# One core, an attention with dilated window beside a state-space scan: a spin on TensorE, a new load order, masks on GpSimd, the scan in two halves and a new order of units

## The chip, the cores and the metric

The kernel runs on one NeuronCore of a Trainium2 chip. The metric is device time of one execution in microseconds (us), lower is better. PE is TensorE, PEld its weight loads, DVE VectorE, ACT ScalarE, POOL GpSimd, SP SyncE, which here issues nearly all DMAs.

## The reference

Two independent computations on sequences of S = 2048 rows with D = 448 features; their outputs stand side by side in the last axis.

```
q, k, v = heads of x @ wqkv                  # A: 16 heads of 28
idx = pos - (0, 2, ..., 14)                  # 8 keys, every second one back
attn = softmax(where(idx >= 0, q . k[idx] * 28**-0.5, -1e9))
a = (attn @ v[idx]) @ wo
Bu = x @ B_bar.T                             # B: complex, 448 states
h[t] = Lam_bar * h[t-1] + Bu[t]
b = 2 * real(h @ C.T) + x * Dskip
```

## The kernel before, in words

**Parity.** All windows step by two, so even and odd rows are kept apart: rows are viewed as 1024 pairs (NK = 1024). xA and xB are loaded transposed (features on partitions), the even half in their first tiles and the odd half in the last ones.

**Attention.** For each parity, `proj_qk` makes 16 units (4 matmuls of 512 columns each, into qT or kT) and `proj_v` 9 units (4 of 448 columns, into Vp). `att_round` is one of 12 rounds per parity (3 query ranges by 4 head groups): 12 mask matmuls (mkB against mkA) and 12 score matmuls into the PSUM tile S, one exponential on ACT into P, 12 matmuls with Vp into av, and a copy into oT. There is one S tile and one av tile. `normalise` sends the sums of each range through DRAM (n1, n2), takes a reciprocal on DVE (n3), sends it back broadcast (n4, n5: inv_b) and multiplies (n6). `wo_block` is the output projection of 128 pairs.

**Scan.** lB is built from Bn and the parameters (`lBa` on ACT, `lBb` on DVE, line 480), transposed on PE and copied into VW (`vwt`, `vwe`). `state_in` (7 matmuls of 512 columns, line 709) makes 14 units, copied into Hs. `scan` turns the complex recurrence into two real ones: it multiplies by tables of cosine and sine (tab, made by POOL products and an ACT sine), runs `tensor_tensor_scan` over 1024 pairs (line 736) and rotates back. There are three such blocks of 128 states and a last one with 64. `y_block` multiplies by CwO and CwEK, which are built from C on ACT and DVE (line 805); `k0` makes the term of the same pair.

**What sets the order.** Nothing in the program is scheduled by hand on the engines: class `Plan` holds every piece as an `Op` with an engine, a duration, dependences and a rank. `run` simulates, takes the lowest rank among what can start, and then emits the instructions in that order. Each engine then executes its own list strictly in that order. Evacuations of PSUM (`evac`) go to ACT or DVE as the plan finds them free. Three PSUM tiles ("mm") turn round for projections, transposes and outputs. Output tiles are four ("yo").

**Start.** SP issues the loads in the order of the `load` calls. ACT issues 13 small DMAs for the parameters, which are laid out one value per partition. DVE builds mkA and mkB in fp32 in some thirty steps (lines 312 to 356). A flag, computed at the end, would start a slow exact path; it does not.

Of the kernel before, what the change touches and what calls it, by code (L numbers as in the profile page):

```python
# [17 lines left out]
QB = 121  # L18
NB = 9
# [15 lines left out]
class Plan:  # L35


    HOP = 0.12
# [10 lines left out]
    def run(self):  # L49
# [4 lines left out]
        while todo:  # L54
            cand = {}
            for op in todo:
                t = 0.0
                for d in op.deps:
                    if d.end is None:
                        t = INF  # L60
                        break
                    t = max(t, d.end + d.lat + (self.HOP if d.ran != op.eng else 0.0))
# [66 lines left out]
def main_part(ctx, tc, A_x, A_wqkv, A_wo, B_x, B_Lambda_re, B_Lambda_im, B_B_re, B_B_im, B_C_re, B_C_im, B_log_dt,  # L129
# [44 lines left out]
    phs = T([128, 4, NK], I32, "oT")  # L174
# [21 lines left out]
    par_raw = T([128, 3, 4], BF16, "par_raw")  # L196
    dsk_raw = T([128, 2, 4], BF16, "dsk_raw")
# [3 lines left out]
    L = {}  # L201

    def load(name, at, q, fn):
        L[name] = P.add(name, q, 0.06, fn, rank=-1000 + len(L), lat=at)

    xA_r = A_x[0].rearrange("(k j) d -> k (j d)", j=2)
    xB_r = B_x[0].rearrange("(k j) d -> k (j d)", j=2)

    for i, vec in enumerate((B_Lambda_re, B_Lambda_im, B_log_dt)):
        def f(i=i, vec=vec):  # L210
            ACT.dma_start(par_raw[:, i, 0:3], vec[0:384].rearrange("(t i) -> i t", i=128))
            ACT.dma_start(par_raw[0:64, i, 3:4], vec[384:448].rearrange("(i o) -> i o", o=1))
# [22 lines left out]
    def bload():  # L235
# [4 lines left out]
        SP.dma_start(Bm[0:64, :], B_B_im[384:448])  # L240
        SP.dma_start(Bm[64:128, :], B_B_re[384:448])
# [12 lines left out]
    load("xA_E0", 4.2, "SP", lambda: xpose(xA, xA_r, 0, 4, 0, 512))  # L254
    for kt in range(4):
        n = 128 if kt < 3 else 64
        load(f"W_Eqk{kt}", 4.5 + 0.6 * kt, "SP",
             lambda kt=kt, n=n: SP.dma_start(raw[0][0:n, kt, 0:D2], A_wqkv[128 * kt:128 * kt + n, 0:D2]))
    load("xA_E1", 9.0, "SP", lambda: xpose(xA, xA_r, 0, 4, 512, 1024))
    load("Bn", 12.0, "SP", bload)  # L260
    load("W_Ev", 13.5, "SP", lambda: wload(0, wv[0], D2, D3))
    load("xB0", 17.0, "SP", lambda: xpose(xB, xB_r, 0, 7, 0, 512))
    load("xB1", 20.0, "SP", lambda: xpose(xB, xB_r, 0, 7, 512, 1024))
    load("xA_O", 24.0, "SP", lambda: xpose(xA, xA_r, 4, 7, 0, 1024))
    load("W_Ov", 26.0, "SP", lambda: wload(1, wv[1], D2, D3))
    load("W_Oqk", 28.0, "SP", lambda: wload(1, raw[1], 0, D2))
    load("wo", 31.0, "SP", woload)
    load("C", 3.0, "SP", cload)
# [4 lines left out]
    o_id = P.add("ident", "POOL", 1.0, c0, rank=-898.5)  # L273
    o_warm = None

    def c1():
        POOL.memset(raw[0][64:128, 3, :], 0.0)
        POOL.memset(raw[0][:, :, D2:900], 0.0)
        POOL.memset(wv[0][64:128, 3, :], 0.0)
        POOL.memset(wv[1][0:64, 0, :], 0.0)  # L280
    o_wz = P.add("wzero", "POOL", 1.5, c1, rank=-899)
# [15 lines left out]
    def c2():  # L297
        POOL.iota(iot, [[1, NK]], base=0, channel_multiplier=0)
    o_iota = P.add("iota", "POOL", 1.0, c2, rank=-898)

    one_i = T([128, 1], I32, "one_i")

    def c3():
        POOL.memset(one_i[:], 1 << 30)
    o_m0 = P.add("mask0", "POOL", 0.5, c3, rank=-897)
    rowi = T([128, 1], I32, "rowi")
    rowf = T([128, 4], F32, "rowf")

# [12 lines left out]

    mf = T([128, 5, 144], F32, "scr")
    mi = mf[:, 4, :].bitcast(I32)

    def c5():

        POOL.iota(mi.rearrange("p (a b) -> p a b", b=8), [[1, 18], [0, 8]], base=-1, channel_multiplier=0)
        V.tensor_copy(mf[:, 0, :], mi)
        POOL.iota(mi.rearrange("p (a b) -> p a b", b=16), [[0, 9], [1, 16]], base=-8, channel_multiplier=0)
        V.tensor_copy(mf[:, 1, :], mi)  # L330
        c = rowf[:, 2:3]
        kind = rowf[:, 1:2]
# [35 lines left out]
    o_wp0 = P.add("wpz", "POOL", 2.0, c7, rank=-898.7)  # L368
# [7 lines left out]
    f32p = T([128, 3, 4], F32, "f32p")  # L376
# [13 lines left out]

    def q1():
        V.tensor_copy(f32p[:], par_raw[:])
    o_q1 = P.add("par_f", "DVE", 0.15, q1, deps=[L["par0"], L["par1"], L["par2"]], rank=-800)
    o_q2 = P.add("dt", "ACT", 0.3, lambda: ACT.activation(dtt[:], ld, ACTF.Exp), deps=[o_q1], rank=-800)

# [12 lines left out]
    o_q3 = P.add("turns", "DVE", 1.0, q3, deps=[o_q2, o_q0], rank=-799)  # L408
# [7 lines left out]
    o_q4 = P.add("rsc", "ACT", 3.0, q4, deps=[o_q3, o_q0], rank=-799)  # L416
# [5 lines left out]
    o_q5 = P.add("lam", "DVE", 0.3, q5, deps=[o_q4], rank=-798)  # L422
# [27 lines left out]
    o_q6 = P.add("coef", "DVE", 2.8, q6, deps=[o_q5], rank=-500)  # L450
# [3 lines left out]
    for t in range(4):  # L454
        def f(t=t):
# [442 lines left out]
    for t in range(4):  # L898
        scan(t, 20 + t)
# [153 lines left out]
```

## Time and profile before

| | |
|---|---|
| time, 2 runs | 186.12 and 188.25, median 187.19 us |
| the profiled execution | 186.38 us, span 184.5 us |
| busy | PE 143.2, DVE 113.3, ACT 104.8, POOL 28.8 us |
| mean granted TensorE clock | 0.928 |

The span runs from the first to the last instruction; the 1.9 us to the device time lie around it. A busy PE is the union of its matmuls, also when they run at half clock.

### The profile page before, as it was taken

Reading aid. Unit: us, or ns where it says so; the run is one execution under the profiler, and the core shown is the slowest. Engines: PE = TensorE matmul, PEld = TensorE weight load, DVE = VectorE, ACT = ScalarE, POOL = GpSimd, SP = SyncE. Lnnn points to the kernel's source line nnn. Section 1 sums busy time; section 2 is a strip of 40 time slices with the busy share of each in tenths; the row PEclk is TensorE's granted clock in tenths of the full one; section 3 lists DMA queues with packets and bytes.
Section 4 is the critical chain, followed back from the end, with each engine's and each line's share of the span. In section 5 each row is a group of like instructions: output and inputs, shape, how many; then the busy total and the mean of one; then the engine's idle time right before and its main releaser. Section 6 shows DMA issues by size and latency. Waiting matters only on the chain.

```text
span 184.5 us, 3726 instructions
## 1 busy us (share of the span) xinstructions
PE 143.2 (78%) x1496; PEld 70.8 (38%) x1504; DVE 113.3 (61%) x219; ACT 104.8 (57%) x157; POOL 28.8 (16%) x40
## 2 busy tenths in 40 slices
PE   0039120589999999999889965599999999999870
PEld 0003020454454444444344433245444455444430
DVE  0058989987050089999999999839833323154420
ACT  0037035777696354379979956885974556312340
POOL 8805507261880000000000000000000000000000
PEclk9999855559999999999999999969999999999997
DMA  4897999900006200000000300130204311333651
GB/s 79 210 189 214 218 206 236 245 14 2 0 0 136 41 0 0 0 0 4 0 9 6 83 0 6 43 97 6 68 10 121 112 56 55 82 102 85 192 166 42
DMA packets 33173, 14.45 MB, mean 78 GB/s; under 512 B 22624, under 2 KB 33152, under 8 KB 33152
## 3 DMA queue, kind: packets, MB, share of 16 engines
q1 hardware_dynamic: 30512, 14.17, 31.5%
q10 hardware_dynamic: 2640, 0.01, 0.8%
q8 instruction: 13, 0.21, 0.5%
q14 instruction: 8, 0.07, 0.1%
HBM read 6.01 MB, written 3.80 MB: 53 GB/s over the span
## 4 chain that ended last, share of the span: by engine, by line
DVE 40%; PE 34%; DMA 11%; ACT 5%; SPq 4%; issue 4%; DVEq 0%; POOL 0%
PE mm L855 12%; DVE scr L736 7%; PE mm L538 6%; PE mm L863 4%; DMA inv_b<-inv 3%; PE mm L709 3%; DVE lB L480 3%; PE mm L683 3%; SPq L657 3%; DMA raw<-in_A_wqkv_dram 3%; DMA par_raw<-in_B_log_dt_dram 2%; DVE scr L731 2%; DVE sm L646 2%; ACT P L606 1%; DVE Hs L732 1%
## 5 line engine op out<-in xcount | busy, mean ns | idle before, releaser
L606 ACT ACTIVATE P<-S 128x1452 bf16<-128x1452 f32 (+1 forms) x24 | 31.5, 1314 | 4.0 <-PE S L597 3.9
L538 PE MATMUL mm<-xA,wqk 128*128 128x512 bf16 x63 | 17.8, 445 | 12.7 <-DVE wqk L287 12.5
L709 PE MATMUL mm<-xB,VW 128*128 128x512 bf16 x96 | 21.2, 379 | 0.1
L538 PEld LDWEIGHTS <-wqk 128*128 128x128 bf16 x64 | 6.9, 110 | 22.9 <-DVE wqk L287 13.4
L490 ACT CAST Hs<-mm 128x512 bf16<-128x512 f32 x14 | 8.2, 585 | 12.0 <-PE mm L709 12.0
L538 PE MATMUL mm<-xA,wqkO 128*128 128x512 bf16 x59 | 14.3, 380 | 0.3 <-issue 0.2
L709 PEld LDWEIGHTS <-VW 128*128 128x128 bf16 x98 | 9.6, 98 | 11.5
L683 PE MATMUL mm<-Wp,oT 128*128 128x448 bf16 x64 | 12.6, 352 | 1.6 <-DMA sm<-sum 1.0
L614 PE MATMUL av<-P,Vp 128*32 128x121 bf16 (+1 forms) x288 | 8.3, 221 | 7.0 <-DVE oT L492 4.3
L736 DVE TENSOR_TENSOR_SCAN scr<-p_r,Hs 128x1024 bf16<-128x1024 f32 x6 | 13.4, 2278 | 0.1
L855 PEld LDWEIGHTS <-Hs 128*128 128x128 bf16 x112 | 10.0, 98 | 9.1 <-issue 2.0
L855 PE MATMUL mm<-CwEK,Hs 128*128 128x448 bf16 x56 | 13.3, 355 | 0.0
L855 PE MATMUL mm<-CwO,Hs 128*128 128x448 bf16 x56 | 13.3, 354 | 0.0
L591 PE MATMUL S<-mkB,mkA 32*128 32x121 bf16 (+1 forms) x288 | 8.3, 219 | 6.4 <-DVE mkB L356 6.4
L490 ACT CAST qT<-mm 128x512 bf16<-128x512 f32 x15 | 9.0, 597 | 6.1 <-PE mm L538 6.0
L490 ACT CAST yo<-mm 128x448 bf16<-128x448 f32 x11 | 5.8, 530 | 11.1 <-PE mm L855 11.1
L492 DVE CAST oT<-av 128x363 bf16<-128x363 f32 (+1 forms) x13 | 6.4, 491 | 7.3 <-PE av L614 7.3
L614 PEld LDWEIGHTS <-Vp 128*32 128x32 bf16 x288 | 4.5, 97 | 16.3 <-issue 8.4
L731 DVE TENSOR_TENSOR scr<-Hs,tab 128x2048 bf16<-128x2048 bf16 x3 | 3.7, 1226 | 11.1 <-ACT Hs L490 10.9
L456 POOL TENSOR_TENSOR oT<-oT,F_i 128x1024 int32<-128x1024 int32 x4 | 7.8, 1942 | 16.7 <-ACT tab L461 16.7
L662 DVE TENSOR_TENSOR oT<-oT,inv_b 128x1452 bf16<-128x1452 bf16 (+1 forms) x6 | 5.2, 871 | 7.2 <-DMA inv_b<-inv 4.6
L560 PEld LDWEIGHTS <-xA 128*128 128x128 bf16 x72 | 6.7, 98 | 6.6 <-issue 0.5
(194 smaller groups left out, 259.5 us busy)
## 6 DMA issues: line engine op xcount, KB each, us to landing
out_dram<-ya SPq DMA_DIRECT2D x16, 112.0 KB, 1.7
out_dram<-yo SPq DMA_DIRECT2D x8, 224.0 KB, 2.4
inv_b<-inv SPq DMA_DIRECT2D x16, 90.8 KB, 2.9
raw<-in_A_wqkv_dram SPq DMA_DIRECT2D x3, 224.0 KB, 3.6
rawO<-in_A_wqkv_dram SPq DMA_DIRECT2D x1, 672.0 KB
inv_b<-inv SPq DMA_DIRECT2D x8, 74.5 KB, 2.2
Wp<-in_A_wo_dram SPq DMA_DIRECT2D x4, 98.0 KB
Bn<-in_B_B_re_dram SPq DMA_DIRECT2D x1, 336.0 KB
```

Source lines behind the costliest of these rows:

```text
L456: POOL.tensor_tensor(phs[:, 1, :], iot, F_i[:, t:t + 1].to_broadcast((128, NK)), ALU.mult)
L490: ACT.copy(dst, src)
L538: PE.matmul(ps[:], Wt[:, j, c:c + 128], xA[:, t0 + j, 512 * blk:512 * blk + 512], start=(j == 0), stop=(j == 3))
L591: PE.matmul(ps[:, i, c:c + n], mkA[p, :], mkB[p, mk:mk + n], start=(c == 0), stop=False, skip_group_check=True)
L606: ACT.activation(pt[:, :, 0:nq], hold["S"][:, :, 0:nq], ACTF.Exp, scale=float(DH) ** -0.5)
L614: PE.matmul(av[32 * i:32 * i + 32, c:c + n], Vp[:, par * NB + b, 4 * g + i, :], hold["P"][:, i, c:c + n], start=True, stop=True, skip_grou ...
L683: PE.matmul(ps[:, 0:D], oT[:, g, par, cols], Wp[:, g, :], start=(g == 0), stop=(g == 3))
L709: PE.matmul(ps[:], VW[:, kt, m, :], xB[:, kt, 512 * blk:512 * blk + 512], start=(kt == 0), stop=(kt == 6))
L731: step("sa", 1.15, lambda: V.tensor_tensor(scr[:], vv, sinb, ALU.mult))
L736: step(f"se{i}", 2.3, lambda i=i: V.tensor_tensor_scan(scr[:, i], r2[:, t:t + 1].to_broadcast((128, NK)), vv[:, i], 0.0, ALU.mult, ALU.add))
L855: PE.matmul(ps[:, 0:D], Hs[:, m, off:off + 128], Cw[:, m, :], start=(m == 0), stop=(m == 6))
L863: PE.matmul(ps[:, 0:D], xB[0:n, j, c0:c0 + 128], CwEK[0:n, 7 + j, :], start=False, stop=False)
```

## The change

- **Spin and parameters.** DVE clears a tile; PE runs 10 matmuls of 512 columns on zeros, then two transposes of the parameters, then two more such matmuls, and only then the first projection. The parameters come by 4 DMAs of 7 rows by 64 values.
- **Loads.** The first x transposes are halved (256 rows), the value weights go ahead of the query and key weights. Bm is copied from Bn by DVE instead of loaded.
- **Masks.** mkA and mkB are made for 32 partitions by 9 `affine_select` and 3 memsets on POOL, and copied to the others by DVE.
- **Scan.** Hs becomes two tiles of 512 pairs. `scan` runs for each half: rotate in, scan, carry (the last state, rotated by the table's entry 512, is the start value `ini` of the second half), rotate out. Tables have 514 columns instead of 1024, in two buffers.
- **Order.** Ranks are new throughout (value units first, state units among attention rounds, attention of the odd parity among y blocks), durations and hop costs of the plan too.

```diff
-    HOP = 0.12
+    HOP = {"PE": 0.28, "SP": 0.05}
...
+    o_z = P.add("zt", "DVE", 0.3, lambda: V.memset(zt[:], 0.0), rank=-2000)
+    P.add("warm0", "PE", 4.2, warm(10), deps=[o_z], rank=-2000)
+    def q0a():
+        ps = ps_mm.tile([128, 28], BF16, tag="mm", name="mmp")
+        hold_w["par"] = ps
+        for h in range(2):
+            PE.transpose(ps[64 * h:64 * h + 64, :], par_raw[:], ident[0:28, 0:28])
+    o_pt = P.add("part", "PE", 0.2, q0a, deps=[L["par3"], o_id], rank=-1999, take="mm")
+    P.add("warm1", "PE", 0.9, warm(2), deps=[o_pt], rank=-1998)
...
+        POOL.affine_select(f, f, u16, ALU.is_gt, NEG, base=0, channel_multiplier=-1)
...
-            POOL.tensor_tensor(phs[:, 1, :], iot, F_i[:, t:t + 1].to_broadcast((128, NK)), ALU.mult)
+            POOL.tensor_tensor(phs[:, b + 1, :], iot, F_i[:, t:t + 1].to_broadcast((128, TB)), ALU.mult)
...
+            def run(i):
+                V.tensor_tensor_scan(scr[:, i], r2[:, t:t + 1].to_broadcast((128, HK)), vv[:, i],
+                                     ini[:, t, i:i + 1] if blk else 0.0, ALU.mult, ALU.add)
+            def carry():
+                e = scr[:, :, HK - 1:HK]
+                TT(ini[:, t, 2:4].unsqueeze(2), e, tab[:, t, 1:2, HK:HK + 1].to_broadcast((128, 2, 1)), ALU.mult)
...
-        state_in(m, blk, -100 + 2 * i + blk)
+            state_in(m, blk, 28 + 1.5 * (7 * blk + i))
...
-                proj_qk(0, blk, g, w, -300 + 20 * blk + 2 * g + w)
+                proj_qk(0, blk, g, w, 9 + 9 * blk + 2 * g + w)
...
-        proj_v(0, b, -240 + b)
-        proj_v(1, b, 100 + b)
-    for t in range(4):
-        scan(t, 20 + t)
+        proj_v(0, b, 5 + b if b < 4 else 15 + b)
+        proj_v(1, b, 58 + b)
+    for blk in range(2):
+        for t in range(4):
+            scan(t, blk, 40 + 20 * blk + 0.1 * t)
```

What stands on SP's queue first, before: xA, the even x, then raw (query and key weights), Bn, and late wvE (value weights).

```order
L224 DMA_TRANSPOSE xA<-in_A_x_dram 128x4x512
L258 DMA raw<-in_A_wqkv_dram 128x896 x3
L258 DMA raw<-in_A_wqkv_dram 64x896
L224 DMA_TRANSPOSE xA<-in_A_x_dram 128x4x512
L236 DMA Bn<-in_B_B_re_dram 128x3x448
...
L240 DMA Bm<-in_B_B_im_dram 64x448
L241 DMA Bm<-in_B_B_re_dram 64x448
L229 DMA wvE<-in_A_wqkv_dram 128x3x448
```

The same queue after the change:

```order
L224 DMA_TRANSPOSE xA<-in_A_x_dram 128x4x256
L229 DMA wvE<-in_A_wqkv_dram 128x3x448
L230 DMA wvE<-in_A_wqkv_dram 64x448
L224 DMA_TRANSPOSE xA<-in_A_x_dram 128x4x256
L258 DMA raw<-in_A_wqkv_dram 128x896 x3
L258 DMA raw<-in_A_wqkv_dram 64x896
L224 DMA_TRANSPOSE xA<-in_A_x_dram 128x4x512
L236 DMA Bn<-in_B_B_re_dram 128x3x448
```

The value weights moved to second place; query and key weights and Bn stand behind them.

DVE, where the first scan block begins, before (scr is the scratch of the scan, Hs the states):

```order
L492 CAST Vp<-mm 128x16x28 x3
L731 TENSOR_TENSOR scr_646<-Hs,tab 128x2048
L732 TENSOR_TENSOR Hs<-Hs,tab 128x2x1024
L733 TENSOR_TENSOR Hs<-Hs,scr_646 128x1024
L734 TENSOR_TENSOR Hs<-Hs,scr_646 128x1024
L736 SCALAR_TENSOR_TENSOR scr_646<-p_r_114,Hs 128x1024 x2
```

The same place after the change, up to where other work comes in between (CwO, the output matrix, and a state unit):

```order
L502 COPY VW<-mmt 128x384 x3
L746 TENSOR_TENSOR scr_681<-Hs_93,tab 128x1024
L747 TENSOR_TENSOR Hs_93<-Hs_93,tab 128x2x512
...
L752 SCALAR_TENSOR_TENSOR scr_681<-p_r_115,Hs_93 128x512 x2
L757 TENSOR_TENSOR ini<-scr_681,tab 128x2
...
L768 COPY Hs_94<-Hs_93 128x2
...
L856 SCALAR_TENSOR_TENSOR CwO<-CT,cfO,ctmp_136 128x448
L502 CAST Hs_94<-mm 128x512
```

The scan now starts right behind the VW copies, in half lengths. All value and all query and key units of the even parity still stand ahead of the state units on PE; from there on state units, attention rounds and DVE's scan run side by side.

## Rows read from the trace of the kernel before

**Rows 1.** The page: busy time, and two lines of 40 slices of 4.6 us

```profile
PE 143.2 (78%) x1496; PEld 70.8 (38%) x1504; DVE 113.3 (61%) x219; ACT 104.8 (57%) x157; POOL 28.8 (16%) x40
...
PEclk9999855559999999999999999969999999999997
...
GB/s 79 210 189 214 218 206 236 245 14 2 0 0 136 41 0 0 0 0 4 0 9 6 83 0 6 43 97 6 68 10 121 112 56 55 82 102 85 192 166 42
```

**Rows 2.** Busy time by stretch: length, PE, PEld, DVE, ACT, POOL, clock, DMA

```profile
11.50:40.60 29.10, 14.25 (x97) 7.88 (x99) 26.81 (x89) 15.05 (x26) 11.43 (x12) 0.67 0.87 198
40.60:58.40 17.80, 17.58 (x83) 8.22 (x83) 7.11 (x16) 13.91 (x18) 9.49 (x7) 0.96 0.09 20
58.40:80.30 21.90, 21.80 (x133) 9.99 (x133) 14.68 (x13) 9.72 (x18) 0.00 (x0) 1.00 0.12 22
80.30:105.00 24.70, 22.84 (x338) 11.12 (x336) 24.13 (x25) 22.34 (x35) 0.00 (x0) 1.00 0.08 18
105.00:120.00 15.00, 8.95 (x206) 5.09 (x208) 14.06 (x28) 10.68 (x18) 0.00 (x0) 1.00 0.06 18
120.00:170.00 50.00, 49.57 (x621) 24.57 (x614) 22.36 (x46) 28.20 (x40) 0.00 (x0) 0.97 0.26 70
170.00:179.00 9.00, 8.23 (x43) 3.96 (x41) 3.12 (x6) 3.63 (x7) 0.00 (x0) 1.00 0.62 180
```

**Rows 3.** Timeline of PE, first 60 us: start, length, instructions

```profile
11.57 1.46 PE L538 MATMUL mm<-xA,wqk 128*128 128x512 bf16 x3 [11.57 <-DVE wqk L287]
...
40.63 10.75 PE L538 MATMUL mm<-xA,wqk 128*128 128x512 bf16 x46 [0.22 <-issue]
51.21 4.70 PE L560 MATMUL mm<-wvE,xA 128*128 128x448 bf16 x24
...
58.38 1.89 PE L709 MATMUL mm<-xB,VW 128*128 128x512 bf16 x7
```

**Rows 4.** Timeline of DVE, first 60 us

```profile
11.02 0.17 DVE L392 CAST f32p<-par_raw 128x12 f32<-128x12 bf16 x1 [11.02 <-DMA par_raw<-in_B_log_dt_dram]
...
15.49 0.17 DVE L407 TENSOR_SCALAR F_i<-p_fr 128x4 int32<-128x4 f32 x1
...
16.32 1.92 DVE L334 TENSOR_SCALAR scr<-scr,rowf 128x128 f32<-128x128 f32 x1
...
25.25 0.23 DVE L356 TENSOR_SCALAR mkB<-scr 128x128 bf16<-128x128 f32 x1
```

**Rows 5.** Groups by line and shape: count, busy us and mean ns, idle before

```profile
L480 DVE SCALAR_TENSOR_TENSOR lB<-Bn,p_lamr,ctmp 128x448 bf16<-128x448 bf16 x7 | 7.4, 1092 | 0.0
...
L805 DVE SCALAR_TENSOR_TENSOR CwO<-CT,cfO,ctmp 128x448 bf16<-128x448 bf16 x7 | 4.5, 672 | 0.0
...
L492 DVE CAST Vp<-mm 128x448 bf16<-128x448 f32 x3 | 1.9, 624 | 0.3
...
L287 DVE COPY wqk<-raw 128x1024 bf16<-128x1024 bf16 x4 | 1.5, 420 | 0.0
```

**Rows 6.** The chain that ended last: start, length, piece

```profile
7.04 3.75 DMA par_raw<-in_B_log_dt_dram
...
65.24 1.24 DVE scr L731
...
77.51 1.24 DVE scr L731
...
159.81 0.20 PE mm L859 x4
...
163.63 0.20 PE mm L859 x4
...
173.41 5.47 PE mm L683 x28
```

**Rows 7.** Timeline of POOL

```profile
4.54 0.29 POOL masks.py:199 TENSOR_SCALAR_AFFINE_SELECT ident<-ident 128x128 bf16<-128x128 bf16 x1
...
16.22 1.93 POOL L456 TENSOR_TENSOR oT<-oT,F_i 128x1024 int32<-128x1024 int32 x1
```

More of the change, by code (lines that the diff above doesn't have):

```diff
@@ L278, in c1 @@
         POOL.memset(raw[0][:, :, D2:900], 0.0)
-        POOL.memset(wv[0][64:128, 3, :], 0.0)
-        POOL.memset(wv[1][0:64, 0, :], 0.0)
-    o_wz = P.add("wzero", "POOL", 1.5, c1, rank=-899)
+    o_wz = P.add("wzero", "POOL", 1.0, c1, rank=-897.5)
+    o_wv = [P.add(f"wvz{i}", "POOL", 0.47, lambda i=i: POOL.memset(wv[i][64 - 64 * i:128 - 64 * i, 3 - 3 * i, :], 0.0),
+                  rank=-899 if i == 0 else -880) for i in range(2)]
     o_rp = [[], []]
@@ L359, in c6 @@
+        POOL.affine_select(c, c, [[0, 144]], ALU.is_ge, 0.0, base=-16, channel_multiplier=1)
+    o_m0 = P.add("mask0", "POOL", 3.5, c3, rank=-600)
+    def c5():
+        V.tensor_tensor(mkB[0:32, :], mk_[:, 0, :], mk_[:, 1, :], ALU.min)
+        for t in (mkA, mkB):
+            V.tensor_copy(t[32:64, :], t[0:32, :])
+            V.tensor_copy(t[64:128, :], t[0:64, :])
+    o_mask = P.add("mask2", "DVE", 0.7, c5, deps=[o_m0], rank=-100)
     def c6():
@@ L389, in main_part, with warm, f @@
     o_q0 = P.add("sg", "POOL", 0.4, q0, rank=-895.5)
-    def q1():
-        V.tensor_copy(f32p[:], par_raw[:])
-    o_q1 = P.add("par_f", "DVE", 0.15, q1, deps=[L["par0"], L["par1"], L["par2"]], rank=-800)
-    o_q2 = P.add("dt", "ACT", 0.3, lambda: ACT.activation(dtt[:], ld, ACTF.Exp), deps=[o_q1], rank=-800)
+    hold_w = {}
+    def warm(n):
+        def f():
+            if not hold_w:
+                hold_w["ps"] = ps_av.tile([128, 512], F32, tag="av", name="warm")
+            for _ in range(n):
+                PE.matmul(hold_w["ps"][:], zt[:, 0:128], zt[:], start=True, stop=True)
+        return f
+    o_z = P.add("zt", "DVE", 0.3, lambda: V.memset(zt[:], 0.0), rank=-2000)
[7 more added lines that the diff above has]
+    P.add("warm1", "PE", 0.9, warm(2), deps=[o_pt], rank=-1998)
+    def q1():
+        ps = hold_w["par"].rearrange("p (v c) -> p v c", c=7)
+        V.tensor_copy(f32p[0:64, :, :], ps[0:64, :, 0:7:2])
+        V.tensor_copy(f32p[64:128, :, 0:3], ps[64:128, :, 1:7:2])
+        V.tensor_copy(f32p[64:128, :, 3:4], ps[64:128, :, 6:7])
+        V.tensor_copy(dskO[0:64, 1:4], ps[0:64, 3, 1:7:2])
+        V.tensor_copy(dskO[64:128, :], ps[64:128, 3, 0:7:2])
+    o_q1 = P.add("par_f", "DVE", 0.8, q1, deps=[o_pt], rank=-990, give="mm")
+    o_q2 = P.add("dt", "ACT", 0.3, lambda: ACT.activation(dtt[:], ld, ACTF.Exp), deps=[o_q1], rank=-990)
     def q3():
@@ L494, in ecost @@
     def ecost(n):
-        return {"ACT": 0.19 + n / 1200.0, "DVE": 0.09 + n / 960.0}
+        return {"ACT": 0.17 + n / 1200.0, "DVE": 0.12 + n / 960.0}
     o_vw = {}
@@ L606, in f @@
             ACT.activation(pt[:, :, 0:nq], hold["S"][:, :, 0:nq], ACTF.Exp, scale=float(DH) ** -0.5)
-        o2 = P.add(f"X{par}{r}{g}", "ACT", 0.2 + 4 * nq / 1200.0, f, deps=[o1] + o_tab, rank=rank - 50, take="P", give="S")
+        o2 = P.add(f"X{par}{r}{g}", "ACT", 0.12 + 4 * nq / 1200.0, f, deps=[o1] + o_tab, rank=rank - 600, take="P", give="S")
         def f():
@@ L690, in f @@
             evac(e, yo[:, 0, :], hold["ps"][:, 0:D])
-        o2 = P.add(f"woe{par}{c}", AD, ecost(448), f, deps=[o1], rank=rank - 40, give="mm", take="yo")
+        o2 = P.add(f"woe{par}{c}", AD, ecost(448), f, deps=[o1], rank=rank - 500, give="mm", take="yo")
         def f():
@@ L713, in f @@
         def f(e):
-            evac(e, Hs[:, m, 2 + 512 * blk:2 + 512 * blk + 512], hold["ps"][:])
-        o_st[m, blk] = P.add(f"ue{m}{blk}", AD, ecost(512), f, deps=[o1, o_vp], rank=rank - 20, give="mm")
-    o_h = []
-    def scan(t, rank):
-        deps = [o_st[m, blk] for m in ((t, t + 3) if t < 3 else (6,)) for blk in range(2)] + [o_tab[t]]
-        last = list(deps) + o_h[-1:]
+            evac(e, Hs[blk][:, m, 2:HK + 2], hold["ps"][:])
+        o_st[m, blk] = P.add(f"ue{m}{blk}", AD, ecost(512), f, deps=[o1, o_vp], rank=rank - 500, give="mm")
@@ L723, in step, with scan @@
+    o_h = [[], []]
+    def scan(t, blk, rank):
+        deps = [o_st[m, blk] for m in ((t, t + 3) if t < 3 else (6,))] + [o_tab[t], o_vp, o_mask]
+        last = list(deps) + (o_h[0] if blk else [])
         def step(name, dur, fn):
-            o = P.add(f"{name}{t}", "DVE", dur, fn, deps=list(last), rank=rank)
+            o = P.add(f"{name}{t}{blk}", "DVE", dur, fn, deps=list(last), rank=rank)
             last[:] = [o]
-        cos, sin = tab[:, t, 0, :], tab[:, t, 1, :]
+        TT = V.tensor_tensor
+        H_ = Hs[blk]
+        cos, sin = tab[:, t, 0, 0:HK], tab[:, t, 1, 0:HK]
+        c5, s5 = tab[:, t, 0, HK:HK + 1], tab[:, t, 1, HK:HK + 1]
@@ new lines, in rot_out @@
+            def rot_out():
+                TT(vv, scr[:], cosb, ALU.mult)
+                TT(scr[:], scr[:], sinb, ALU.mult)
+                TT(vv[:, 0], vv[:, 0], scr[:, 1], ALU.subtract)
+                TT(vv[:, 1], vv[:, 1], scr[:, 0], ALU.add)
+                if blk == 0:
+                    V.tensor_copy(Hs[1][:, t:t + 4:3, 1:2], H_[:, t:t + 4:3, HK + 1:HK + 2])
+            step("sr", 2.1, rot_in)
+            step("s0", 1.2, lambda: run(0))
+            step("s1", 1.2, lambda: run(1))
@@ new lines, in rot_out @@
+            def rot_out():
+                TT(scr[:, 1, :], scr[:, 1, :], sin, ALU.mult)
+                TT(vv, scr[:, 0, :], cos, ALU.mult)
+                TT(vv, vv, scr[:, 1, :], ALU.subtract)
+                if blk == 0:
+                    V.tensor_copy(Hs[1][:, 6, 1:2], H_[:, 6, HK + 1:HK + 2])
+            step("sr", 1.6, rot_in)
+            step("s0", 1.7, run)
+            if blk == 0:
+                step("sc", 0.5, carry)
+            step("so", 1.15 + 0.15 * (1 - blk), rot_out)
@@ L923, in f @@
         PE.matmul(ps[0:1, 0:1], csum[:, 0:1], csum[:, 1:2], start=True, stop=True)
-    o2 = P.add("fl1", "PE", 0.2, f, deps=[o1, o_one], rank=190, take="mm")
+    o2 = P.add("fl1", "PE", 0.2, f, deps=[o1, o_one], rank=110, take="mm")
     def f():
         V.tensor_scalar(flag[:], hold_f["ps"][0:1, 0:1], float(H * S) - 0.5, None, ALU.is_lt)
-    P.add("fl2", "DVE", 0.1, f, deps=[o2], rank=190, give="mm")
+    P.add("fl2", "DVE", 0.1, f, deps=[o2], rank=110, give="mm")
     P.run()
```

313 lines of the change are left out of this document (146 added, 167 removed).

## The prediction

> **What bounds the kernel now.** Read the busy line and the slices of the page first. PE is busy 143.2 of 184.5 us, more than any other engine, and the line of the granted clock shows fives in slices 4 to 8; DMA traffic fills the same stretch and falls from 245 to 14 GB/s after slice 8, at about 37 us [rows 1]. So there are two kernels in one: a head in which data and parameters arrive, and a body in which PE works. The stretches give the sizes [rows 2]. From 11.5 to 40.6 us PE is busy 14.25 of 29.1 us at a mean clock of 0.67, while DVE is busy 26.8: the head is DVE's. Its timeline says why: the parameters come only at 11.02, and then the steps of the two masks stand on it from 16.32 to 25.48 [rows 4], ahead of everything that leads to VW. In the timeline of PE, 46 query and key matmuls can start only at 40.63, the value units at 51.21, the first state unit at 58.38 [rows 3].
>
> The body runs from 58.4 to 179.0 us. PE's busy times in it are 21.80 + 22.84 + 8.95 + 49.57 + 8.23 = 111.4 of 120.6 us [rows 2]; so 9.2 us are idle, 6.05 of them between 105 and 120, where DVE is busy 14.06 of 15 and PE's copies wait behind the scan in DVE's queue. The tail behind PE's last matmul, 173.41 + 5.47 [rows 6], is 184.5 - 178.9 = 5.6 us.
>
> The time is therefore: start of the first state unit + PE work from there + idle in it + 5.6, and 1.9 us around the span (186.38 - 184.5). The profiled execution is 0.8 us under the median of the runs shown, so I take its sum as it is.
>
> **The head, part by part.** *Parameters.* In the chain the last of nine DMAs of the three parameter vectors is issued at 7.04 and lands 3.75 us later [rows 6]. Four in place of thirteen are issued by 7.04 x 4/9 = 3.1 us and land at about 6.9; the two transposes and the spin stand ahead of the first value unit on PE, which has nothing to do before 11.57 anyhow [rows 3]. If the DMAs land late the value units wait behind the transposes in PE's queue; I price that at 0 to 2 us. From the first parameter step to F_i took 11.02 to 15.66 with other steps between [rows 4]; with the extra casts out of PSUM I take 3.0 us, so F_i at 9.9 instead of 15.7.
>
> *Loads.* Query and key weights now stand behind the value weights: 0.4 MB more ahead at 0.21 MB per us [rows 1] is 1.9 us later. What hides it is DVE, which behind F_i has three copies of value units (0.62 each), four of weights (0.42) [rows 5] and 0.4 us of small steps: 9.9 + 4.0 = 13.9 us for the first query and key unit, 2.3 us later than today. This edit alone loses; it pays because four value units are already done. Bn comes behind 3.05 MB, about 16.5 us after the start of transfers, still ahead of its use.
>
> *PE from 13.9 us.* Sixteen query and key units at 4 x 10.75/46 = 0.93 (14.9 us), five value units at 4.70/6 = 0.78 (3.9) [rows 3], two attention rounds (about 1.5) and the transposes for VW (4 us, an estimate from the 14.25 us that PE is busy in the head of today with 16 such matmuls, a round and all transposes). Sum 24.3: the first state unit at 38.2, against 58.4.
>
> *DVE in the same stretch.* Of today's 26.8 us, masks (9.2, and about 1.2 for their row numbers) go to POOL, parameters and weights come earlier (3.6), and lB drops from 1092 to about 672 ns apiece, the figure of the same shape in CwO (7 x 0.42 = 2.9) [rows 5]; eight more evacuations (5.0), more VW copies (1.5), diagonals, Bm and mask copies (3.4) come in, estimates from like steps. That is some 20 us: 33.9, so PE is the later one, by 4 us.
>
> *Masks on POOL.* No row shows these shapes; the nearest is the affine select of the identity, 0.29 us [rows 7], and thirteen steps are about 3.5 us, ahead of the table products, with half of today's length. What they may cost is DVE: a mask step took 1.92 us beside POOL's product of 1.93 us from 16.22, and its like 0.23 once POOL was idle [rows 4, 7]. POOL's products still sum to 8 x 0.97 = 7.8 us, so the bounds are 0 and 7.8 on DVE. With 4 us of slack there I take 1 us on the path. The Trainium skill (SBUF — State Buffer, Who interferes with whom) says that one of the two engines waits for the other's whole instruction, but not when DVE has at most one input in SBUF and runs outside its two-port modes; evacuations out of PSUM would then pass freely, the loss would stay inside the 4 us of slack, and the sum would be 1 us lower. The 1.92 us agree with its first half; for the second no row stands here.
>
> I put the first state unit at 39 us, with bounds of 36 and 44.
>
> **The body.** PE's work is today's 111.4, less about 1.0 (one round is done earlier), less 1.5 for the clock of 0.97 over 50 us [rows 2]: 108.9. The halves of the scan add nothing to PE. *DVE:* a block of two rows of states takes 77.51 - 65.24 = 12.3 us today [rows 6]. Three of these and the short one are 45; twice as many instructions, carries and copies add about 5 (an estimate of 0.07 us on some 70 instructions). Beside it the new order puts fourteen steps for CwO and CwEK (9.4), the reciprocals and products of three ranges (6, an estimate from their size beside a CwO step) and some twenty evacuations (0.62 each, 13) [rows 5] on DVE: 78 us from the first scan to the last. It starts when two state units are copied, 4 us after the first: 43 + 78 = 121. PE reaches the first y block of the second half after 108.9 less 3.5 pairs of y units (3.82 each, 163.63 - 159.81), ten output blocks (5.47/7 = 0.78 each) [rows 6] and the first y unit itself, that is 85.7 us: 39 + 85.7 = 124.7. So the halves do what they can: the scan is 4 us ahead of its reader, with PE at full work. But two engines near 100% with strict queues disturb each other, and that is the term that no row fixes. From below it is 1 us (PE from 120 to 170 idles 0.4 of 50), from above 17 (the 6.05 of 15 between 105 and 120, over half of the stretch) [rows 2]. I take 7.5, near today's 9.2, since odd-parity projections and rounds beside a busy DVE are what idled 1.86 of 24.7 us.
>
> Sum: 39 + 108.9 + 7.5 + 5.6 = 161.0, with 1.9 **162.9 us**, 13% under today.
>
> **Rivals.** *All covers hold:* idle 1 instead of 7.5, first state unit at 37: 154.4. For it speaks the full PE from 120 to 170; against it, 105 to 120. *The head's clock or POOL:* the spin ends before data come, PE idles until 13.9, and the units run at the lower level (1.2 GHz) as the head does today, with clock 0.67 [rows 2]; 18.8 us of units with a third at half clock cost 6 us; POOL's 7.8 us on DVE give about the same: 169. Against it: the units behind today's transposes lost only 0.7 us to the clock (0.96 over 17.8 us from 40.6) [rows 2]. *Lock-step, the slower one:* DVE's evacuations stand behind scan steps all through the 85.7 us, and PE works at the share of 105 to 120, 8.95/15 = 0.60: 143 in place of 85.7 + 7.5, so 213 us. It decides against the change (over 190.9) when PE's share there is under 85.7/121 = 0.71. Against it: the new order takes evacuations between the scan steps, and ACT, which shares the evacuations, is busy only 70.9 of the 111.6 us from 58.4 to 170 today [rows 2].
>
> **How the numbers follow.** Two per cent is about what a measurement of this kernel can tell from no change: 183.4 to 190.9. Chances: forecast, 157 to 167, 0.50; covers hold 0.20; head at 167 to 172, 0.18; some lock-step, 172 to 183, 0.05; within 2% 0.03; lock-step beyond 0.04. The range takes the covers' value less 1.4 and the head's case with two us of idle more: 153 to 174.
>
> **What would show it.** First value matmul at 6 to 8 us and first state unit at 36 to 42; full clock from about 17 us; DVE free of masks; between the first state unit and the first y unit of the second half PE at 90% or more; the last scan step a few us ahead of that y unit; a tail of 5 to 6. The forecast is wrong if DVE's last scan step ends after 128, if PE's share in the body is under 85%, or if the first state unit is not before 44.

## The result, and the profile after

167.25 and 168.68 us, median 167.97, against 187.19: ratio 0.897, 95% interval 0.870 to 0.925. The forecast was 162.9, its own band 157 to 167; the time lies in the band of the rival "the head's clock or POOL" (167 to 172), and in the range. The profiled execution is the one of 167.25 us, span 165.5 us.

The page after, the lines of [rows 1]:

```profile
PE 145.0 (88%) x1518; PEld 69.7 (42%) x1518; DVE 124.6 (75%) x271; ACT 92.8 (56%) x144; POOL 24.9 (15%) x49
...
PEclk9997898799999999999999999999999999997898
```

PE does the same work in 19 us less. Busy times by stretch (columns as in [rows 2]):

```profile
10.00:15.00 5.00, 1.53 (x4) 0.42 (x5) 4.96 (x11) 0.43 (x3) 4.51 (x10) 0.92 1.02 268
15.00:20.00 5.00, 5.00 (x19) 2.01 (x18) 4.79 (x19) 2.64 (x5) 3.84 (x5) 0.74 1.10 210
20.00:25.00 5.00, 2.68 (x12) 1.05 (x11) 4.87 (x12) 3.57 (x6) 3.89 (x6) 1.00 1.13 238
25.00:30.00 5.00, 3.39 (x12) 1.41 (x12) 4.67 (x16) 2.80 (x4) 0.00 (x0) 0.78 0.99 230
...
46.70:80.00 33.30, 33.30 (x371) 15.44 (x370) 28.58 (x54) 24.54 (x37) 3.98 (x4) 1.00 0.18 38
80.00:131.90 51.90, 51.90 (x767) 26.28 (x766) 49.09 (x99) 37.83 (x58) 0.00 (x0) 1.00 0.15 42
131.90:145.00 13.10, 13.10 (x89) 6.50 (x88) 6.41 (x14) 2.12 (x4) 0.00 (x0) 1.00 0.27 75
145.00:159.70 14.70, 12.45 (x55) 5.39 (x53) 6.19 (x13) 2.97 (x6) 0.00 (x0) 0.88 0.52 151
```

From 46.7 to 145 us PE is never idle, though DVE is busy 91% of the time up to 131.9. The loss is ahead of 46.7, while DVE is all but full. PE there (as [rows 3]; in brackets the idle time and what ended it):

```profile
6.43 3.19 PE L570 MATMUL mm<-wvE,xA 128*128 128x448 bf16 x16 [0.86 <-DMA wvE<-in_A_wqkv_dram]
...
14.64 6.16 PE L548 MATMUL mm<-xA,wqk 128*128 128x512 bf16 x21 [1.06 <-DVE wqk L286]
22.16 1.89 PE L548 MATMUL mm<-xA,wqk 128*128 128x512 bf16 x8 [1.37 <-DVE kT L502]
26.61 2.40 PE L548 MATMUL mm<-xA,wqk 128*128 128x512 bf16 x8 [2.57 <-DVE kT L502]
...
39.45 0.35 PE L624 MATMUL av<-P,Vp 128*32 128x121 bf16 x12 [2.10 <-ACT P L616]
...
46.67 7.72 PE L719 MATMUL mm<-xB,VW 128*128 128x512 bf16 x35
...
131.90 0.35 PE L901 MATMUL mm<-CwO,Hs 128*128 128x448 bf16 x1
...
150.51 5.62 PE L693 MATMUL mm<-Wp,oT 128*128 128x448 bf16 x20 [1.87 <-DVE flag L974]
156.52 3.19 PE L693 MATMUL mm<-Wp,oT 128*128 128x448 bf16 x16 [0.38 <-ACT ya L500]
```

Two waits, 1.37 and 2.57 us, are for casts of kT, which last 0.69 us each. DVE's timeline (as [rows 4]) tells why they come late (the 128x4 steps from L429 on, the "coefficient steps", work out cfO and cfE, the factors of CwO and CwEK):

```profile
9.47 0.25 DVE L411 TENSOR_SCALAR F_i<-p_fr 128x4 int32<-128x4 f32 x1
...
12.47 2.11 DVE L286 COPY wqk<-raw 128x1024 bf16<-128x1024 bf16 x2
14.50 1.00 DVE L429 TENSOR_SCALAR p_nr<-p_lamr 128x4 f32<-128x4 f32 x1
15.42 0.15 DVE L430 TENSOR_TENSOR p_den<-f32p 128x4 f32<-128x4 f32 x1
15.49 1.01 DVE L431 TENSOR_TENSOR p_tA<-f32p 128x4 f32<-128x4 f32 x1
...
21.42 0.69 DVE L502 CAST kT<-mm 128x512 bf16<-128x512 f32 x1
22.02 0.69 DVE L331 TENSOR_TENSOR mkB<-mk__108 32x144 bf16<-32x144 bf16 x1
22.72 1.86 DVE L333 COPY mkA<-mkA 32x128 bf16<-32x128 bf16 x1
...
25.87 0.69 DVE L502 CAST kT<-mm 128x512 bf16<-128x512 f32 x1
...
131.10 0.42 DVE L801 TENSOR_TENSOR Hs<-Hs,scr 128x512 bf16<-128x512 bf16 x1
```

Most steps of 128x4 values last 0.15 us, some 0.80 to 1.02. POOL (as [rows 7]) runs eight phase products, of which the first and the last pair are, with the memset behind them:

```profile
13.26 1.03 POOL L462 TENSOR_TENSOR oT<-oT,F_i 128x514 int32<-128x514 int32 x1
14.37 1.10 POOL L463 TENSOR_TENSOR oT<-oT,one_i 128x514 int32<-128x514 int32 x1
...
21.59 1.04 POOL L462 TENSOR_TENSOR oT<-oT,F_i 128x514 int32<-128x514 int32 x1 [0.78 <-ACT tab L467]
22.71 1.04 POOL L463 TENSOR_TENSOR oT<-oT,one_i 128x514 int32<-128x514 int32 x1
23.69 0.85 POOL L290 MEMSET rawO<- 64x900 bf16 x1
```

A long step ends when the product beside it ends: 14.50 + 1.00 against 14.37 + 1.10. The mkA copy (22.72 + 1.86) ends with the memset behind the last product (23.69 + 0.85). The casts of kT read PSUM and keep their 0.69 us even beside a product (21.42 beside 21.59).

Of the experiments, e2, e9 and e10 were profiled in an execution over 1.5% above the fastest of their kernel, so their first state units below are, if anything, late; the ratios below leave such executions out, the medians do not.

### The profile page after: what moved, and what is told of

It is laid out like the page before. It is cut to its first block, busy times and chain, and to the rows that moved or that the text cites. A ratio compares the mean times of both kernels' runs of the same rounds, so it can differ in the third digit from the quotient of the medians.

```text
span 165.5 us, 3791 instructions
## 1 busy us (share of the span) xinstructions
PE 145.0 (88%) x1518; PEld 69.7 (42%) x1518; DVE 124.6 (75%) x271; ACT 92.8 (56%) x144; POOL 24.9 (15%) x49
## 4 chain that ended last, share of the span: by engine, by line
PE 67%; DVE 14%; DMA 6%; ACT 5%; SPq 3%; issue 1%; DVEq 0%; ACTq 0%
PE mm L548 14%; PE mm L719 13%; PE mm L901 9%; PE mm L570 7%; PE mm L693 5%; PE av L624 4%; DMA inv_b<-inv 4%; PE S L601 3%; PE mm L881 3%; SPq L667 3%; PE mm L909 3%; DMA out_dram<-yo 2%; PE warm L377 2%; PE S L607 2%; DVE wqk L286 2%; ACT P L616 2%
## 5 line engine op out<-in xcount | busy, mean ns | idle before, releaser
L693 PE MATMUL mm<-Wp,oT 128*128 128x448 bf16 x64 | 15.0, 386 | 2.2 <-DVE flag L974 1.9
L548 PE MATMUL mm<-xA,wqkO 128*128 128x512 bf16 x64 | 15.5, 380 | 0.0
L500 ACT CAST yo<-mm 128x448 bf16<-128x448 f32 x9 | 4.8, 532 | 16.1 <-PE mm L901 8.8
L500 ACT CAST ya<-mm 128x448 bf16<-128x448 f32 x12 | 6.1, 535 | 12.8 <-DMA out_dram<-yo 11.5
L500 ACT CAST qT<-mm 128x512 bf16<-128x512 f32 x10 | 5.9, 586 | 9.7 <-PE mm L548 9.7
L500 ACT CAST Hs<-mm 128x512 bf16<-128x512 f32 x12 | 7.0, 586 | 7.4 <-PE mm L719 7.3
L693 PEld LDWEIGHTS <-oT 128*128 128x128 bf16 x64 | 6.4, 105 | 9.2 <-issue 4.8
L570 PE MATMUL mm<-wvE,xA 128*128 128x448 bf16 x36 | 8.6, 378 | 0.9 <-DMA wvE<-in_A_wqkv_dram 0.9
L500 ACT CAST oT<-av 128x363 bf16<-128x363 f32 (+1 forms) x18 | 8.0, 445 | 1.7 <-PE av L624 1.7
L548 PEld LDWEIGHTS <-wqkO 128*128 128x128 bf16 x64 | 5.8, 98 | 6.6
```

The source lines that it names most:

```text
L500: ACT.copy(dst, src)
L548: PE.matmul(ps[:], Wt[:, j, c:c + 128], xA[:, t0 + j, 512 * blk:512 * blk + 512], start=(j == 0), stop=(j == 3))
L570: PE.matmul(ps[:, 0:D], xA[:, t0 + j, ks:ks + 128], Wt[:, j, :], start=(j == 0), stop=(j == 3))
L693: PE.matmul(ps[:, 0:D], oT[:, g, par, cols], Wp[:, g, :], start=(g == 0), stop=(g == 3))
```

## The experiments

All were timed in five rounds (e3 three); e0 to e3 ran together, so did e4 to e7, e8 and e9, e10 and e11. "us faster" below is the difference of two ratios times 187.2.

```
run                 median us  ratio to before, 95%        first state unit (us)
e0_changed            167.56   0.8925 (0.8851-0.8999)      47.05
e1_coef_late          159.89   0.8587 (0.8552-0.8621)      40.99
e2_small_products     161.41   0.8658 (0.8615-0.8701)      41.99
e3_y_waits_both       173.49   0.9302 (0.9241-0.9363)      47.10
e4_no_spin            167.42   0.8949 (0.8896-0.9003)      46.62
e5_qk_first           170.70   0.9136 (0.9077-0.9196)      50.07
e6_tail               161.36   0.8632 (0.8576-0.8688)      40.23
e7_old_masks          170.29   0.9107 (0.9047-0.9166)      49.81
e8_norm_bufs          156.01   0.8359 (0.8310-0.8407)      40.66
e9_split_copies       158.26   0.8403 (0.8341-0.8464)      41.65
e10_norm_no_spin      155.21   0.8299 (0.8246-0.8351)      43.08
e11_spin_gap          154.42   0.8266 (0.8226-0.8307)      38.32
```

**e0.** 

> The changed kernel again, unaltered, so that the variants beside it have a time on the same chip: 167 to 169 us, ratio 0.89 to 0.905 of the kernel before, first state unit at 46 to 47 us.

As expected.

**e1: the small steps out of the casts' way.**

```diff
+    o_q6.deps.append(o_lB[-1]); o_mask.deps.append(o_ph[-1])
-    o_dg = P.add("dg", "DVE", 1.4, f, deps=[o_q1, o_id, o_dz], rank=22)
+    o_dg = P.add("dg", "DVE", 1.4, f, deps=[o_q1, o_id, o_dz, o_lB[-1]], rank=22)
```

> The coefficient steps (L429 to L453) and the diagonal matrices (L865 to L868) are made to wait for the last lB step, the mask copies (L331 to L334) for the last of GpSimd's phase products; nothing is left out. Theory (in the head, the casts of the Q/K projections stand in VectorE's queue behind small steps that GpSimd's products stretch, 7.0 us of coefficient steps and 3 us of mask steps, and TensorE waits 1.4 + 2.6 us for two kT casts): those two waits go, the first state unit comes at 42 to 43.5 us instead of 46.7, and the time falls by 3 to 4 us, unless VectorE's 4 us of work put into the body make the second half's first y unit wait, which would give 1 to 3 of them back. Rival (TensorE's head is set by the landing of the loads and by ScalarE, so that another wait is next in line): first state unit at 46 us or later, time within 1 us of the changed kernel.

6.3 us faster. PE in e1, with no wait for kT left:

```profile
14.64 10.94 PE L548 MATMUL mm<-xA,wqk 128*128 128x512 bf16 x37 [1.06 <-DVE wqk L286]
...
40.99 7.72 PE L719 MATMUL mm<-xB,VW 128*128 128x512 bf16 x35
...
144.62 3.94 PE L693 MATMUL mm<-Wp,oT 128*128 128x448 bf16 x20 [1.66 <-DVE flag L974]
150.20 3.19 PE L693 MATMUL mm<-Wp,oT 128*128 128x448 bf16 x16 [1.63 <-ACT ya L500]
```

The theory holds, and was undersized: the new order also has other units beside the first exponential, so the 2.10 us at 39.45 are gone. A cast out of PSUM that started just behind a product, in e1 on DVE and POOL:

```profile
18.70 0.69 DVE L502 CAST qT<-mm 128x512 bf16<-128x512 f32 x1 [4.12 <-PE mm L548]
```

```profile
18.61 1.04 POOL L462 TENSOR_TENSOR oT<-oT,F_i 128x514 int32<-128x514 int32 x1 [1.01 <-ACT tab L467]
```

It kept its 0.69 us.

**e2: the products shortened, the order kept.**

```diff
-            POOL.tensor_tensor(phs[:, b + 1, :], iot, F_i[:, t:t + 1].to_broadcast((128, TB)), ALU.mult)
+            POOL.tensor_tensor(phs[:, b + 1, 0:8], iot[:, 0:8], F_i[:, t:t + 1].to_broadcast((128, 8)), ALU.mult)
```

> GpSimd's eight phase products (L462, L463) are cut from 514 columns to 8, and ScalarE's sine reads one column repeated, so the rotation table is wrong; the order of the instructions on TensorE, VectorE and ScalarE is unchanged. Theory (the same instructions on VectorE are long only because GpSimd's products run beside them): no 128x4 step over 0.3 us, the coefficient steps 3 us instead of 7.0, the mkA copy 0.2 us instead of 1.86, the double wqk copy 0.8 to 1.0 us instead of 2.1, first state unit at 41.5 to 43 us, time 4 to 5 us under the changed kernel. Rival (the steps are slow for another reason, such as the copies and casts around them, or the wait is for ScalarE and loads): steps stay at 0.8 to 1.0 us, or they shrink and the first state unit still comes at 46 us, time within 1 us.

5.0 us faster. The steps of DVE in e2 that took 1.00 and 1.86 us:

```profile
13.50 0.16 DVE L429 TENSOR_SCALAR p_nr<-p_lamr 128x4 f32<-128x4 f32 x1
...
19.12 0.18 DVE L333 COPY mkA<-mkA 32x128 bf16<-32x128 bf16 x1
```

So the same instructions in the same order are long only beside GpSimd's work. From the double weight copy (12.47) to the first state unit DVE's 69 instructions take 27.1 us in the changed kernel and 20.3 in e2: the products cost DVE 6.8 us. The queue (e1) and the length (e2) are two ends of one loss.

**e3: the first half's y units planned behind the scan.**

```diff
-            deps = o_h[c // 4] + o_h[0] + ([o_dg] + o_cwO if par else o_k0 + o_cwE)
+            deps = o_h[1] + o_h[0] + ([o_dg] + o_cwO if par else o_k0 + o_cwE)
```

> Every y unit waits for both halves of the scan; nothing is left out, and the scan itself stays in two halves with its carry. Theory (the halves pay by letting 15 us of y units of the first half run on TensorE while VectorE scans the second): TensorE runs out of work some 11 to 14 us before the scan ends at 131 us, and the time rises to 177 to 182 us. Rival (TensorE is the bound anyway and other units, the output projections above all, fill the place): time within 2 us of the changed kernel.

7.1 us slower, between the two. The edit does less than its label says: the plan moves the units back, but on the chip a y unit still waits only for the half that it reads (the first starts at 125.57, the scan ends at 132.7). What is lost is their place between the attention rounds, which then stand bare. PE in e3, one such round of four (their waits sum to 5.4 us) and the first y unit, then DVE's last scan step:

```profile
118.61 0.32 PE L624 MATMUL av<-P,Vp 128*32 128x121 bf16 x12 [1.43 <-ACT P L616]
...
125.57 0.56 PE L901 MATMUL mm<-CwO,Hs 128*128 128x448 bf16 x1
```

```profile
132.25 0.42 DVE L801 TENSOR_TENSOR Hs<-Hs,scr 128x512 bf16<-128x512 bf16 x1
```

**e4: no spin.**

```diff
-    P.add("warm0", "PE", 4.2, warm(10), deps=[o_z], rank=-2000)
+    P.add("warm0", "PE", 4.2, warm(0), deps=[o_z], rank=-2000)
```

(and `warm1` alike)

> The twelve spin matmuls (L377) are left out of the changed kernel; nothing of the result depends on them. Theory (the spin buys TensorE's clock for the units that come right behind it): the sixteen matmuls of the first value units run at the lower clock level, their casts on VectorE and the weight copies behind those come 1 to 1.5 us later, the Q/K units start at half clock as well, and the time rises by 1.5 to 3.5 us. Rival (TensorE waits for the weight copies until 14.6 us in any case, so slow value units are hidden there): time within 1 us of the changed kernel.

The rival's time: no difference (intervals overlap). Its reason, a start at 14.6 in any case, does not hold. PE in e4:

```profile
6.38 5.45 PE L570 MATMUL mm<-wvE,xA 128*128 128x448 bf16 x16 [1.22 <-DMA wvE<-in_A_wqkv_dram]
...
15.71 10.88 PE L548 MATMUL mm<-xA,wqk 128*128 128x512 bf16 x36 [0.57 <-DVE wqk L286]
...
29.04 1.02 PE L548 MATMUL mm<-xA,wqk 128*128 128x512 bf16 x4 [1.70 <-DVE qT L502]
```

The value units take 5.45 instead of 3.19 us, the query and key (Q/K) stream starts 1.07 us later and runs at a granted clock of 0.50 from 15 to 20. But the two waits for kT (3.94 us) are gone, and one of 1.70 for a qT cast stands in their place: the last products now meet the diagonals (dgE and dgO, L865 to L868) and no longer the mask copies ahead of a kT cast. So a loss and a gain of like size met; that the spin is worthless by itself does not follow from e4.

**e5: Q/K units first.**

```diff
-        proj_v(0, b, 5 + b if b < 4 else 15 + b)
+        proj_v(0, b, 15 + b)
```

(and the load of `W_Ev` behind `xA_E2`)

> The value weights are loaded behind the last part of the even x, and the four value units that stood first take their place among the others (ranks 15 to 18); nothing is left out. Theory (as the prediction had it: the order costs the Q/K units 2.3 us and pays 3.1 us of value units done): Q/K units stream from 11.5 to 13 us instead of 14.6, TensorE does nothing before them, and the time changes by 0 to 2 us upwards. Rival (value units first are worth what they fill): 3 to 4 us slower.

The rival: 3.9 us slower. Three matmuls start at 10.23, the stream at 15.82, 1.2 us later than with the value units first, because diagonals had taken the free place in DVE's queue ahead of the fourth weight copy:

```profile
12.48 1.87 DVE L868 TENSOR_SCALAR dgO<-ident,dskO 128x128 bf16<-128x128 bf16 x3
...
15.35 0.41 DVE L286 COPY wqk<-raw 128x1024 bf16<-128x1024 bf16 x1
```

DVE did not wait before that copy, so the landing of the weights was not what set it.

**e6: the end.**

```diff
-        P.add(f"n5{k}", "SP", 0.3, f, deps=[o4, last_nm[0]], rank=rank, lat=3.0)
+        P.add(f"n5{k}", "SP", 2.0, f, deps=[o4, last_nm[0]], rank=rank, lat=3.0)
```

(also 0.5 for the single transfers, eight yo buffers, the flag in the `av` bank)

> On top of e1_coef_late: eight output buffers instead of four, the flag's matmul in the bank of the attention output instead of one of the three shared ones, and the planner's durations of SyncE's transfers set to what the trace shows (0.5 us for one, 2.0 for the four of inv_b); nothing is left out. Theory (the two idle stretches of TensorE at the end, 1.7 + 1.6 us in e1_coef_late, are waits for buffers held by copies that stand in VectorE's and ScalarE's queues behind transfers): both fall under 0.5 us and the time goes 2 to 3.3 us under e1_coef_late. Rival (the end is set by the chain of transfers of the last normalisation): under 1 us.

The rival: 0.8 us slower than e1, intervals overlapping. The buffers no longer bind, the last normalisation does, behind SP's output sends. PE in e6:

```profile
151.04 3.87 PE L693 MATMUL mm<-Wp,oT 128*128 128x448 bf16 x12 [3.27 <-DVE oT L672]
```

**e7: the old masks.**

```diff
-    o_mask = P.add("mask2", "DVE", 0.7, c5, deps=[o_m0], rank=-100)
+    o_mask = P.add("mask2", "DVE", 4.0, c5, deps=[o_m1], rank=-399)
```

(`c3` to `c5` as before the change)

> The masks are built as in the kernel before (21 steps on VectorE and two iotas), in a buffer of their own; all else is the changed kernel, nothing is left out. Theory (what the masks on GpSimd bring is that VectorE's queue is free ahead of the weight copies): the mask steps take 6 to 9 us in front of the weight copies, the Q/K units stream from 18 to 22 us instead of 14.6, and the time rises by 4 to 7 us. Rival (the phase products start at F_i, 3.5 us sooner, and are over when the coefficient steps come, so that these run at their short length and pay the masks back): time within 2 us of the changed kernel.

3.4 us slower, in between: eight long mask steps stand beside the products and a memset, and the Q/K units start at 23.19, later than the theory had them, but the coefficient steps behind them are short. DVE in e7, a step beside a product and one after the last:

```profile
12.88 1.03 DVE L338 TENSOR_TENSOR mfo<-mfo 128x128 f32<-128x128 f32 x1
...
19.29 0.29 DVE L346 TENSOR_TENSOR mfo<-mfo 128x128 f32<-128x128 f32 x1
```

**e8: normalisations side by side.**

```diff
-        sm = Late([16 * nch, 3, ncl], BF16, "sm", f"sm{k}")
+        sm, inv_b = Late([16 * nch, 3, ncl], BF16, f"sm{k % 3}", f"sm{k}"), invs[k % 2]
```

> On top of e1_coef_late, with its planner's durations: three buffers for the sums (sm) and two for their spread inverses (inv_b) in place of one each, so that the transfers of a normalisation need not wait for the one before it; seven output buffers and the flag in the attention output's bank as in e6_tail. Nothing is left out. Theory (what e6_tail left: the end is set by three normalisations that run one behind the other through four transfers each): the last product with inv_b, at 148.9 us in e1_coef_late and 150.2 in e6_tail, comes at 141 to 144, TensorE's two idle stretches near the end fall from 3.3 us to under 0.8, and the time goes 2.5 to 3.5 us under e1_coef_late. Rival (one chain's transfers, or SyncE's queue, take that long by themselves): last product at 147 or later, time within 1 us of e1_coef_late.

4.3 us faster than e1, more than the theory had. The last product, on DVE, and PE's last stretch in e8:

```profile
141.60 0.78 DVE L672 TENSOR_TENSOR oT<-oT,inv_b 128x1192 bf16<-128x1192 bf16 x1 [0.82 <-DMA inv_b<-inv]
```

```profile
142.46 6.98 PE L693 MATMUL mm<-Wp,oT 128*128 128x448 bf16 x36
```

**e9: weight copies on two engines.**

```diff
-        o_rp[0].append(P.add(f"rpE{kt}", "DVE", 0.35, f, deps=[L[f"W_Eqk{kt}"], o_wz], rank=-950 + kt))
+        o_rp[0].append(P.add(f"rpE{kt}", "DVE" if kt % 2 else "ACT", 0.45 if kt % 2 else 1.0, f, deps=[L[f"W_Eqk{kt}"], o_wz], rank=-950 + kt))
```

> On top of e8_norm_bufs: two of the four copies of the Q/K weights go to ScalarE, which is idle from 10.4 to 15.3 us, and GpSimd's first phase product waits for the last of them. Nothing is left out. Theory (the stream of Q/K units starts when the last weight copy is done, at 14.6 us, and two of these copies take 2.1 us together beside GpSimd's product): the last copy is done at 12 to 12.8 us, the stream starts there, the first state unit comes 1.5 to 2.5 us earlier and the time falls by as much against e8_norm_bufs. Rival (the loads of weights or of x, or the copies out of the accumulators, then set the pace): first state unit within 0.7 us of e8_norm_bufs, time the same.

The rival: no gain (intervals overlap). The stream does start at 12.37, 2.3 us earlier, but new waits follow, 1.48 us for a kT cast and 1.72 for the first exponential. Which of them decides stays open.

**e10 and e11: the spin again, with the casts free.** e10 has the edit of e4 on e8; e11 adds:

```diff
+                if (par, blk, g, which) == (0, 0, 0, 0):
+                    warm((6, 2, 6, 6)[j])()
```

> e8_norm_bufs without the twelve spin matmuls (L377); nothing of the result depends on them. Theory (in e4_no_spin the slow units were hidden only by the waits for kT, and these are gone now): the last weight copy comes 1 us later and more of the Q/K units run at the lower clock, so the first state unit comes at 42 to 44 us instead of 40.7 and the time rises by 1.5 to 3 us. Rival (TensorE's idle 3.4 us between value units and Q/K units undo what the spin gave in any case): first state unit within 0.7 us, time within 0.8 us of e8_norm_bufs.

> e8_norm_bufs with twenty more spin matmuls, put ahead of each of the four matmuls of the first Q/K unit, where TensorE waits for the weight copies (1.4 + 0.5 + 1.1 + 0.8 us); nothing of the result depends on them. Theory (the granted clock of 0.54 from 15 to 20 us is what those waits cost): the clock stays at 1.0, the 37 matmuls of the stream take 8 us instead of 10.6, the first state unit comes at 38 to 39.5 us instead of 40.7 and the time falls by 1 to 2.5 us. Rival (with a faster stream the casts of VectorE and ScalarE, or lB, are next in line, as in e9_split_copies): first state unit at 40.2 us or later, time within 0.8 us of e8_norm_bufs.

e10: the time does not rise, against the theory; its interval overlaps that of e8. Its first state unit, 43.08, lies where the theory had it, but in an execution of 159.74 us, and what the others did in the head is not on record. e11 is 1.7 us faster than e8, intervals just apart (0.8307 and 0.8310), on another chip. The stretch behind the weight copies, in e8 and then in e11 (columns as above):

```profile
15.00:20.00 5.00, 5.00 (x14) 1.85 (x13) 1.22 (x3) 2.13 (x3) 3.83 (x5) 0.54 1.09 233
```

```profile
15.00:20.00 5.00, 5.00 (x25) 2.27 (x24) 2.47 (x4) 4.08 (x6) 4.70 (x5) 1.00 1.09 231
```

With the gap filled the clock stays at its upper level and 25 matmuls go where 14 went. In time e11 cannot be told from e10, so that a spin pays at all here is not shown. e11 has the lowest ratio of the versions tried, 0.827.

## Why the prediction was right, and where it was off

The parts of the sum, for the profiled execution: first state unit 46.7 (39 forecast), PE work of the body 33.3 + 51.9 + 13.1 + 12.45 = 110.75 (108.9), idle in it 2.25 (7.5), tail 5.8 (5.6), around the span 1.75 (1.9). So +7.7, +1.85, -5.25, +0.2 and -0.15 make the 4.35 us between 162.9 and 167.25.

That the miss is no larger is in part luck: two errors of opposite sign met. The head came 7.7 us late, past its own bound of 44, and the idle term was 5.25 us too large; with 7.5 us of idle time the same head would have given 172.5. Of the three signs of a wrong forecast two showed: the first state unit came after 44 (46.7) and the last scan step after 128 (131.5). The third, a share of PE under 85%, did not.

- **The step that failed** is "With 4 us of slack there I take 1 us on the path", in the head. DVE's 33.9 us were set against PE's 38.2 as one sum, but DVE works its queue in order: the coefficient steps (7.0 us, from 14.5 to 21.4) and the masks' copies stood ahead of two kT casts that PE needed at once. Nor was there slack: the sum of some 20 us for DVE's steps behind 13.9 is what e2 shows without the long products (20.3), and with them it is 27.1. The bound of 7.8 us was thus the right size for the products' price of 6.8, and 1 us was not: shortening the products (e2) brings the first state unit forward by some 5 us, moving the steps (e1) by 6.1.
- **The rule cited** from the Trainium skill (SBUF — State Buffer, Who interferes with whom) is borne out in both halves: a step of 0.15 us took 1.0 beside a product of 1.04, and casts out of PSUM kept their 0.69 (21.42 in the changed kernel, 18.70 in e1). (L429 has one input in SBUF and waited too; by the rule it ran in a two-port mode, which no row shows.) The conclusion drawn from it, 1 us less, is not: the free casts stood behind steps that were not free.
- **The clock** was the smaller part of the rival. Full clock "from about 17 us" did not come: the granted clock was 0.74 from 15 to 20 and 0.78 from 25 to 30 us. With the waits gone (e8), filling the gap (e11) brings the first state unit from 40.7 to 38.3, where the waits were worth 6.0 (46.7 to 40.7). In e11 PE needs 38.32 - 14.77 = 23.6 us from the start of the stream, where 24.3 were forecast: the sum of PE's head was right, its covers were not.
- **Small terms.** First value unit 6.43 (6 to 8). F_i 9.47 (9.9), by two errors that cancel: parameters on PE at 4.84, not 6.9, and then 4.4 us of steps instead of 3.0, one of 1.69 us beside a memset on POOL. Masks on POOL took from 8.34 to 13.29, 4.95 us instead of 3.5, in twelve steps and not thirteen. The order that "pays because four value units are already done" comes to 3.1 - 2.3 us by the prediction's figures; undoing it costs 3.9 (e5), as the 2.3 are not lost: DVE's queue, not the landing, sets the start of the Q/K units. In [rows 1] the fives stand in slices 6 to 9, not 4 to 8; no sum rests on that.
- **The body.** The lock-step did not come, and neither did the 7.5 us of disturbance: no idle time while DVE scans. The +1.85 of PE work is nearly all clock: behind the idle 1.87 us at the end, 20 matmuls took 5.62 us (granted clock 0.53 from 150.5 to 154), where the same 20 in e1, behind 1.66 us, took 3.94 at 1.00; why the clock fell in the one and not in the other stays open. PE reached the second half's first y unit 85.2 us after the first state unit (85.7 forecast); the scan took 81.0 us instead of 78 (from 50.5) and ended at 131.5, 0.4 us ahead of it. That it ended after 128, a sign of "wrong", follows from the late head. e3 shows what the order of units gives there: y units between the rounds hide exponentials of 1.2 to 1.4 us, and without them the kernel is 7.1 us slower, 5.4 of it in four bare rounds. What the scan's halves give apart from that was not tried; a scan in one piece would have been needed.
- **The idle 2.25 us** lie at the end, ahead of 150.51 and 156.52, a wait that no term of the sum had. e6 and e8 show that it was not a matter of output buffers but of three normalisations, one behind the other, that shared one buffer for sums and one for inverses.

## What to carry to other kernels

When two engines are compared by sums, ask for each short step on the fuller one what stands behind it in the queue and who waits for that; work without a deadline (coefficients, masks, diagonals) belongs behind the casts. Beside GpSimd's products a small step of VectorE in SBUF cost 1.0 us instead of 0.15, until the product ended; keep both out of the same stretch or shorten GpSimd's. A wait at the end that names a buffer may only cover the next one; look for what would be ready last if the buffer were free.

## What was not expected of the hardware

- In the changed kernel a float32 step of four columns on VectorE took 0.80 to 1.02 us when it met a GpSimd product of 1.04 to 1.10, and 0.13 to 0.18 us without (e2). Each of the eight products held up one instruction, so one step in several was hit.
- Leaving out twelve spin matmuls ahead of the data raised neither time (e4, e10). In e8, which has them, the granted clock is 0.54 right after the 5.1 us (9.5 to 14.65) in which PE issued three matmuls.
